# Reordering the opening loads of a four-layer kernel: fourth tile behind the seventh weight chunk

## Chip, cores, metric

One core of one Trainium2 chip. The metric is device time of one execution in microseconds (us), lower is better. The granted TensorE clock was 1.0, as a mean over the whole execution.

Engines: PE = TensorE matmul, DVE = VectorE, ACT = ScalarE, POOL = GpSimd, SP = SyncE, which issues all loads here (its queue shows as SPq).

## The reference, cut

Four layers over x of 2048 rows by 1024, bf16: linear attention, gated product, and both again. Each layer normalises its input first.

```python
x = x + _A_ref(_layernorm(x), A_wqkv, A_wo)          # phi(q), phi(k), kv = pk^T v, o = num / den, @ wo
x = x + _B_ref(_layernorm(x), w_gate, w_up, w_down)  # (x @ w_gate) * (x @ w_up) @ w_down
# ... and both once more
```

The change touches only the start of the first layer: loading x and the k weights, normalising the first four row tiles of 128 rows, and the first products.

## The kernel before

All loads go through one queue, in program order:

```python
load_x(0)
load_x(1)
for k in range(0, 3):
    load_k(k, k + 1)          # one 128x1024 chunk (256 KB) of the k weights
load_x(2)
load_k(3, 4)
load_x(3)
for k in range(4, 8):
    load_k(k, k + 1)
```

The first four tiles are only centred before their product; the reciprocal deviation is applied later, as a scale in the exponential on ACT. Tiles 0 and 1 are transposed on PE, 2 and 3 by DMA (`turn`). Two ways to a mean matter for tiles 2 and 3:

```python
def mean_by_halves(t, i):     # half on ACT, half on DVE
    nc.scalar.activation(out=junk[:, 0:NB], in_=X[:, t, 0:NB], func=ACT.Copy, scale=1.0 / D,
                         accum_out=part[:, i:i + 1])
    nc.vector.tensor_scalar(out=junk[:, NB:D], in0=X[:, t, NB:D], scalar1=1.0 / D, scalar2=0.0,
                            op0=ALU.mult, op1=ALU.add, accum_out=part[:, i + 1:i + 2])
# ... (cut)
mean_by_halves(2, 2)
centre_by_halves(2, 2)
turn(XN[:, 2, :], 0, 2)
ln_stats(3)                                  # the full statistics, on DVE
centre(3, stat[3][0][:, 0:1])
turn(XN[:, 3, :], 0, 3)
load_q()                                     # q weights, two loads of 1 MB
for t in range(4, NT):
    load_x(t)
for t in range(3):
    ln_stats(t)
for k in range(3, 6):
    for t in range(2):
        k_part(t, k, k + 1)                  # product of tile t with chunk k
for t in range(2):
    k_part(t, 6, 8)
k_part(2, 0, 8)
k_part(3, 0, 8)
# ... (cut) then q_unit(0): tile 0's q product, eight steps of two matmuls
```

## Time and profile before

| | us |
|---|---|
| median, first 3 runs | 1622.09 (1621.53 to 1622.28) |
| profiled span | 1620.1 |
| PE busy | 1607.5 (99%) |
| wait of PE at the fifth weight chunk | 0.38 in this trace |

The opening is the only part of this kernel where PE waits for a load at all; the lines that show it are in the prediction. How to read such a case: PE is the chain, so only PE's start-to-start gaps count, and a "true" wait below is a step less the 0.216 us that the prediction works out; the profile's own "idle before" is smaller by 0.16.

### The profile page before, as it was taken

The page shows a single profiled execution, that of the slowest core. Times are in us where ns is not written, and L with a number is a line of the kernel's source. Part 1 is how long each engine was busy: PE and PEld are TensorE (multiplying, and loading weights), DVE is VectorE, ACT ScalarE, POOL GpSimd, SP SyncE. Part 2 cuts the span into 40 slices and gives each one's busy share as a digit, 9 for nine tenths or more (in the row PEclk, how much of TensorE's full clock was granted, in tenths as well). Part 3 has the DMA queues.
Part 4 walks back from the last instruction along what each step waited for, and adds up shares of the span by engine and source line. Part 5 has one row for each costly group of instructions (what it writes and reads, how often), then busy time and mean ns, then how long its engine had stood idle before and what let it go on. Part 6 is the DMA issues. An engine that isn't in the chain of part 4 may idle for free.

```text
span 1620.1 us, 18047 instructions
## 1 busy us (share of the span) xinstructions
PE 1607.5 (99%) x7710; PEld 734.5 (45%) x7861; DVE 616.6 (38%) x946; ACT 284.0 (18%) x384; POOL 54.5 (3%) x135
## 2 busy tenths in 40 slices
PE   9999999999999999999999999999999999999999
PEld 4444444444444444444444444444444444444444
DVE  6899853202311321243255798432123113211111
ACT  5522201101110110011045231011011101101110
POOL 2100000000000000010000000000000000000000
DMA  8224856512650552142420257655236306521400
GB/s 247 53 72 93 246 162 176 162 52 60 171 159 0 147 162 81 52 156 66 92 52 1 78 114 219 181 157 165 69 102 175 127 20 173 165 66 65 156 1 26
DMA packets 236719, 183.10 MB, mean 113 GB/s; under 512 B 102368, under 2 KB 217312, under 8 KB 236640
## 3 DMA queue, kind: packets, MB, share of 16 engines
q1 hardware_dynamic: 236640, 181.95, 39.0%
q8 instruction: 61, 1.00, 0.3%
q14 instruction: 18, 0.15, 0.0%
HBM read 153.09 MB, written 4.19 MB: 97 GB/s over the span
## 4 chain that ended last, share of the span: by engine, by line
PE 99%; issue 1%; DMA 0%; SPq 0%; DVE 0%
PE ps L196 50%; PE ps L538 48%; PE ps L565 1%; DMA W<-in_A_wqkv_dram 0%; PE kv L306 0%; SPq L109 0%; PE pm L328 0%; PE ps L328 0%; DVE X L546 0%
## 5 line engine op out<-in xcount | busy, mean ns | idle before, releaser
L538 PE MATMUL ps<-xT,R 128*128 128x512 bf16 x2382 | 525.9, 379 | 2.6
L538 PEld LDWEIGHTS <-R 128*128 128x128 bf16 x2432 | 238.0, 98 | 286.9
L542 DVE TENSOR_TENSOR R<-gs,ps 128x512 bf16<-128x512 f32 x224 | 153.9, 687 | 533.5 <-ACT gs L541 533.5
L196 PEld LDWEIGHTS <-R 128*128 128x128 bf16 x2248 | 220.0, 98 | 265.2
L541 ACT COPY gs<-ps 128x512 f32<-128x512 f32 x224 | 131.3, 586 | 1040.2 <-PE ps L538 1011.5
L538 PE MATMUL ps<-xT,W 128*128 128x512 bf16 x1130 | 250.4, 379 | 1.2
L196 PEld LDWEIGHTS <-xT 128*128 128x128 bf16 x1536 | 149.5, 98 | 181.4 <-issue 1.9
L196 PE MATMUL ps<-W,xT 128*128 128x512 bf16 x997 | 222.8, 379 | 1.9 <-issue 0.3
L538 PEld LDWEIGHTS <-W 128*128 128x128 bf16 x1152 | 112.7, 98 | 135.9
L196 PE MATMUL ps<-W,R 128*128 128x512 bf16 x733 | 170.1, 379 | 0.8
L546 DVE TENSOR_TENSOR X<-X,ps 128x1024 bf16<-128x1024 bf16 (+3 forms) x34 | 39.4, 1158 | 335.8 <-PE ps L196 282.8
L196 PE MATMUL ps<-R,R 128*128 128x512 bf16 x506 | 111.8, 379 | 0.4
L196 PE MATMUL ps<-PQ,R 128*128 128x512 bf16 x488 | 111.4, 379 | 0.5
L196 PE MATMUL ps<-R,xT 128*128 128x512 bf16 x502 | 110.3, 379 | 0.5
L201 ACT ACTIVATE e<-ps 128x1024 bf16<-128x1024 f32 x56 | 57.3, 1024 | 141.2 <-PE ps L196 86.0
L175 DVE BATCH_NORM_STATS2 st<-X 128x6 f32<-128x512 bf16 x128 | 81.7, 680 | 0.1
L179 POOL TENSOR_SCALAR ve<-mv 128x1 f32<-128x1 f32 x64 | 16.2, 254 | 1325.8 <-DVE mv L177 1325.8
L196 PE MATMUL ps<-GL,R 128*128 128x512 bf16 x240 | 57.8, 379 | 0.3
L196 PE MATMUL ps<-xT,R 128*128 128x512 bf16 x240 | 57.5, 379 | 0.2
L378 DVE TENSOR_TENSOR X<-X,ps 128x1024 bf16<-128x1024 bf16 x32 | 38.7, 1209 | 17.0 <-PE ps L196 17.0
L186 DVE TENSOR_SCALAR R<-X,mv,rstd 128x1024 bf16<-128x1024 bf16 x64 | 33.7, 542 | 27.3 <-POOL rstd L181 24.0
L205 DVE TENSOR_SCALAR e<-e 128x1024 bf16<-128x1024 bf16 x64 | 26.9, 421 | 38.1 <-ACT e L201 38.1
(73 smaller groups left out, 456.6 us busy)
## 6 DMA issues: line engine op xcount, KB each, us to landing
R<-in_B_w_gate_dram SPq DMA_DIRECT2D x38, 1024.0 KB, 5.4
R<-in_B_w_up_dram SPq DMA_DIRECT2D x38, 1024.0 KB, 7.6
W<-in_B_w_gate_dram SPq DMA_DIRECT2D x18, 1024.0 KB, 5.4
W<-in_B_w_up_dram SPq DMA_DIRECT2D x18, 1024.0 KB, 7.6
W<-in_A_wqkv_dram SPq DMA_DIRECT2D x10, 1024.0 KB, 6.2
W<-in_B_w_down_dram SPq DMA_DIRECT2D x6, 1024.0 KB, 11.2
X<-in_A_x_dram SPq DMA_DIRECT2D x16, 256.0 KB, 6.7
PQ<-in_B_w_down_dram SPq DMA_DIRECT2D x4, 1024.0 KB, 8.4
```

The costliest lines, as they stand in the source:

```text
L175: nc.vector.bn_stats(out=st[:, c, :], in_=X[:, t, c * NB:(c + 1) * NB])
L179: nc.gpsimd.tensor_scalar(out=ve[:], in0=mv[:, 1:2], scalar1=1e-5, scalar2=None, op0=ALU.add)
L186: nc.vector.tensor_scalar(out=dst, in0=X[:, t, :], scalar1=mv[:, 0:1], scalar2=rstd[:], op0=ALU.subtract, op1=ALU.mult)
L196: nc.tensor.matmul(out=ps[:, n, :], lhsT=lhsT, rhs=rhs[:, n * NB:(n + 1) * NB], start=start, stop=stop)
L201: nc.scalar.activation(out=e[:], in_=flat(ps), func=ACT.Exp, **sc)
L205: nc.vector.tensor_scalar(out=e[:], in0=e[:], scalar1=1.0, scalar2=EPS, op0=ALU.min, op1=ALU.add)
L378: nc.vector.tensor_tensor(out=X[:, t, :], in0=X[:, t, :], in1=flat(ps), op=ALU.add)
L538: nc.tensor.matmul(out=ps[:, n, :], lhsT=w[:, k, j * P:(j + 1) * P], rhs=xT[g % 2][:, k, :], start=(k == 0), stop=(k == KD - 1))
L541: nc.scalar.copy(out=gs[:], in_=ps[:, 0, :])
L542: nc.vector.tensor_tensor(out=hT[:, f, :], in0=gs[:], in1=ps[:, 1, :], op=ALU.mult)
L546: nc.vector.tensor_tensor(out=X[:, t, a:b], in0=X[:, t, a:b], in1=ps, op=ALU.add)
L565: nc.tensor.matmul(out=ps[:, 0, 0:b - a], lhsT=hT[:, f, tl * P:(tl + 1) * P], rhs=wd[f][:, a:b], start=(f == 0), stop=(f == KF - 1))
```

## The change

Its intent: the wait at the fifth chunk comes from tile 3 standing ahead of it in the queue, so move tile 3 behind the seventh chunk; make up for its lateness with the quicker mean; use DVE's free time for tile 0's statistics; let the last steps of tiles 0 and 1 alternate, so that the eighth chunk is wanted later.

```diff
-    for k in range(0, 3):
+    for k in range(8):
         load_k(k, k + 1)
-    load_x(2)
-    load_k(3, 4)
-    load_x(3)
-    for k in range(4, 8):
-        load_k(k, k + 1)
+        if k in (2, 6):
+            load_x(2 if k == 2 else 3)
...
-            part = small.tile([P, 4], F32, tag="part", bufs=1, name="part")
+            part = small.tile([P, 6], F32, tag="part", bufs=1, name="part")
...
-            ln_stats(3)
-            centre(3, stat[3][0][:, 0:1])
+            ln_stats(0)
+            mean_by_halves(3, 4)
+            centre_by_halves(3, 4)
             turn(XN[:, 3, :], 0, 3)
...
-            for t in range(3):
+            for t in range(1, 4):
                 ln_stats(t)
-            for k in range(3, 6):
+            for k in range(3, 8):
                 for t in range(2):
                     k_part(t, k, k + 1)
-            for t in range(2):
-                k_part(t, 6, 8)
```

## The prediction

> **What bounds the kernel now.** I began with the page: is there anything but the matrix engine to win from?
>
> ```profile
> span 1620.1 us, 18047 instructions
> ...
> PE 1607.5 (99%) x7710; PEld 734.5 (45%) x7861; DVE 616.6 (38%) x946; ACT 284.0 (18%) x384; POOL 54.5 (3%) x135
> ...
> PE 99%; issue 1%; DMA 0%; SPq 0%; DVE 0%
> ```
>
> The first row gives the busy times, the last the chain that ended last. The chain is PE almost throughout, so a microsecond that PE loses or wins anywhere in the opening goes to the end undiminished, and nothing else counts. The diff touches the first 25 us only. So I next asked for the chain in the first 60 us (start, length, what):
>
> ```profile
> 4.48 5.72 DMA W<-in_A_wqkv_dram
> 10.20 0.04 issue
> 10.24 2.10 PE ps L196 x9
> 12.35 0.05 issue
> 12.40 10.74 PE ps L196 x49
> 23.14 0.05 issue
> 23.19 10.74 PE ps L196 x49
> ```
>
> Reader's points: a weight chunk issued at 4.48 lands at 10.20, PE starts on it at 10.24, and from there runs without a break. From 12.40 to 23.19 there are 49 records and one that is missing (each "issue 0.05" is such a hole), so one matmul takes 10.79 / 50 = 0.216 us. All waits of PE from 9 us to the end are these:
>
> ```profile
> PE ps L196 <- issue: 0.3, 2, 0.2
> PE ps L196 <- DMA W<-in_A_wqkv_dram: 0.2, 1, 0.2
> ```
>
> So one wait is left to remove, the one at 10.24. How long is it really? The timeline of PE before it:
>
> ```profile
> 7.92 2.10 PE L196 MATMUL ps<-W,xT 128*128 128x512 bf16 x9
> 10.24 0.38 PE L196 MATMUL ps<-W,xT 128*128 128x512 bf16 x1 [0.22 <-DMA W<-in_A_wqkv_dram]
> ```
>
> The profile counts 0.22 because it lets a matmul last 0.38, but the next could start 0.216 after the last. The ninth starts at 7.92 + 8 x 0.216 = 9.65, so the tenth could have started at 9.86: 0.38 us lost. That is the whole prize, 0.02% of the span.
>
> **What the skill says.** "TensorE: Matmul & The Clock Gate", Back-to-back issue gap, gives N/2.4 + 2.5 ns for a warm isolated gap, 215.8 ns at N = 512; the trace agrees (0.216). The lower sustained figure for N = 512 given there, about 131 ns, is not seen here. "DMA: Bandwidth & Descriptors", Queues, rings and completion order, says that each DMA engine consumes descriptors in ring order: with one issuing queue, to move a transfer in the queue is to exchange landing times. The trace agrees; the 256 KB transfers of the opening land one after another about 0.67 us apart. "Perfetto Trace Analysis", DMA Instruction — HWDGE, says that the recorded issue starts when its semaphores are satisfied and excludes the transfer: so I take landings, not the ends of issues.
>
> **The change part by part.**
>
> *Order of loads.* Issue times stay, since every one of the twelve transfers is 256 KB; contents change. Landings, as issue plus time to landing (queried issue by issue): slot 7 at 3.53 + 5.3 = 8.8, slot 8 at 4.01 + 5.5 = 9.5, slot 9 at 10.20, slot 10 at 4.96 + 5.9 = 10.9, slot 11 at 5.58 + 6.0, finer 11.53, slot 12 at 6.62 + 5.6 = 12.25. Before, tile 3 held slot 8 and the fifth to eighth chunks slots 9 to 12. After, the fifth chunk holds slot 8, the sixth 9, the seventh 10, tile 3 slot 11, and the eighth chunk keeps 12.
> PE wants the fifth at 9.86 (there at 9.5), the sixth four matmuls later at 10.72 (10.20), the seventh at 11.59 (10.9). With the k steps alternating, the eighth is wanted at 12.45 (12.25); by the old order, both last steps of tile 0 together, at 12.02, a wait of some 0.27. So alternation is needed, and adds no matmul. Gain: -0.38 us, with 0.2 us to spare at the tightest weight chunk.
>
> *Tile 2* is as before: its transpose is issued at 9.60 and lands 3.6 later at 13.2, wanted at 13.69 - 0.38 = 13.31. Just in time.
>
> *Tile 3's mean.* Tile 2 goes through the same code now, so its durations are known (DVE, then ACT):
>
> ```profile
> 8.21 0.69 DVE L415 TENSOR_SCALAR_CACHE_REDUCE junk<-X 128x512 bf16<-128x512 bf16 x1 [1.00 <-DMA X<-in_A_x_dram]
> 8.82 0.08 DVE L415 DVE_READ_ACCUMULATOR junk<-X 128x1 f32 x1
> 9.02 0.55 DVE L419 TENSOR_SCALAR R<-X,part 128x1024 bf16<-128x1024 bf16 x1
> 9.54 1.28 DVE L175 BATCH_NORM_STATS2 st<-X 128x6 f32<-128x512 bf16 x2
> 10.86 0.21 DVE L177 BATCH_NORM_AGGREGATE mv<-st 128x2 f32<-128x12 f32 x1
> 11.10 0.49 DVE L394 TENSOR_SCALAR R<-X,mv 128x1024 bf16<-128x1024 bf16 x1
> ```
>
> From the landing at 8.18 to the transpose at 9.60: 1.42 us. Tile 3 landed at 9.51 before, but its statistics and centring ran on DVE from 9.54 to 11.59. After, tile 0's statistics fill 9.54 to 11.07, tile 3 lands at 11.53, and its transpose is issued at 11.53 + 1.42 = 12.95 rather than 11.61: 1.34 later. It landed 3.1 after its issue; then 16.05, wanted at 17.15 - 0.38 = 16.77. In time, by 0.7.
>
> *Tile 0's statistics first* let ACT begin tile 0's exponential at about 13.1 instead of 14.02, where it waited for the reciprocal deviation. PE did not wait for that buffer before (nothing in its list), so this gives PE nothing; DVE ends its fourth statistics near 17.1 instead of 15.6, which PE does not see either.
>
> *What stands behind tile 3 in the queue.* The issuing queue takes its instructions in order:
>
> ```profile
> 9.60 3.25 SPq L190 DMA_TRANSPOSE xT<-R  x2
> 12.90 1.15 SPq L109 DMA_DIRECT2D W<-in_A_wqkv_dram  x2
> 14.09 1.26 SPq L109 DMA_DIRECT2D X<-in_A_x_dram  x2
> ```
>
> The two 1 MB halves of the q weights follow tile 3's transpose. The second is issued at 13.52, and the issue's own view has its landing:
>
> ```profile
> W<-in_A_wqkv_dram SPq DMA_DIRECT2D x1, 1024.0 KB, 7.7
> ```
>
> 13.52 + 7.7 = 21.2. The first lands at 12.90 + 5.6 = 18.5. Tile 0's q product wants the second for its fifth step. From 12.40: six matmuls to tile 2, 16 for tile 2, 16 for tile 3, 8 for q's first four steps: 12.40 + 46 x 0.216 = 22.33. Slack before: 1.1 us. After, both issues are 1.34 later, the halves land at 19.9 and 22.57, and PE, 0.38 earlier, wants them at 20.22 and 21.95. The first is in time; the second is late by 22.57 + 0.04 - 21.95 = 0.66 us.
>
> Sum: -0.38 + 0.66 = +0.28 us. I expect one wait to be exchanged for a longer one: 1622.09 + 0.28 = 1622.37, given as 1622.35.
>
> **The rivals.**
> 1. The q weights come in time and the whole 0.38 is kept: 1621.7. For it: the transposes of tiles 2 and 3 no longer overlap, so the engines may be quieter; in the 1 us windows from 14 to 16 us, traffic was only 100 and 266 GB/s, near 395 later, so something held the q weights back which the change may remove. Against: that weak stretch is just the end of tile 3's transpose (landing 14.76), which moves with it. Chance 1 in 4, partial recovery included.
> 2. Tile 3's transpose becomes the wait, if its landing takes over 3.8 us: +0.1 to +0.5 at tile 3, but this pushes PE towards the late q weights, and the two waits do not add: 1622.4 to 1622.6. Against: 3.1 in the profile here.
> 3. The eighth chunk or tile 2 slips by 0.1 to 0.2. Such a small wait also comes out of the later q wait, so the end is unchanged as long as the q wait stands: 1622.35 again.
> 4. The earlier exponential lets PE gain more. Against: no PE wait on ACT exists to remove.
>
> **Range and chances.** All branches lie within 1 us of the old time; the three runs of before spread over 0.75 us, more than the effect. So the range is 1621.6 to 1623.0, and a 2% move (32 us) would need something outside the opening, which the diff doesn't touch.
>
> **What would show it.** In the new profile: no wait at 10.24, PE dense from about 6.8 to 21.9; transposes issued near 9.60 and 12.95; the q loads issued near 14.24 and 14.86; then a PE wait on the wqkv load near 22, shown as about 0.5 (0.66 less the 0.16 that the modelled ends hide). Step 1 is wrong if a wait near 10 to 12 us remains; the last if PE runs through 22 us dense, and then the time should fall to about 1621.7.

## The result, and the profile after

| | median | runs |
|---|---|---|
| before, same rounds | 1621.95 | 6 (1621.53 to 1622.28) |
| after | 1622.35 | 6 (1621.78 to 1622.65) |

The ratio is 1.0002, 95% interval 0.9989 to 1.0015. Ratios are the mean time of one kernel's fast runs over that of the other's of the same rounds, so not quite the ratio of the medians. By the 2% measure nothing happened.

The queue of loads and transposes after (start, length, count), in answer to the one the prediction shows:

```profile
9.30 4.54 SPq L187 DMA_TRANSPOSE xT<-R  x2
13.89 1.15 SPq L109 DMA_DIRECT2D W<-in_A_wqkv_dram  x2
15.08 11.34 SPq L109 DMA_DIRECT2D X<-in_A_x_dram  x12
```

The q weights are issued at 13.89 in place of 12.90. This execution's opening loads ran about 0.3 us early (tile 2 landed at 7.88, before at 8.18), so relative to them the shift is the 1.3 us foretold. DVE, in answer to the lines of before:

```profile
9.19 1.28 DVE L172 BATCH_NORM_STATS2 st<-X 128x6 f32<-128x512 bf16 x2
11.22 0.69 DVE L412 TENSOR_SCALAR_CACHE_REDUCE junk<-X 128x512 bf16<-128x512 bf16 x1 [0.51 <-DMA X<-in_A_x_dram]
12.04 0.55 DVE L416 TENSOR_SCALAR R<-X,part 128x1024 bf16<-128x1024 bf16 x1
```

Tile 0's statistics come first, then DVE waits 0.51 us for tile 3, which lands at 11.19 and is centred for a transpose issued at 12.61: 1.42 us. And the waits of PE from 5 us to the end:

```profile
PE pt L400 <- DVE R L416: 0.5, 1, 0.5
PE ps L193 <- issue: 0.3, 2, 0.2
```

The wait at the fifth chunk is gone, as foretold, and the one for the q weights is not in the list either. The single matmul records show a step of 0.288 in place of 0.216 at the fifth q step, 22.11, just after the landing at 22.07: a wait of 0.07 us, too short for the list. Taken alone, this trace speaks for the prediction's first rival (q weights in time). But this profile is of the fastest of the six runs, 1621.78. A trace of a typical one was needed.

### The profile page after: what moved, and what is told of

Its sections match the earlier page's. It is cut to its first block, busy times and chain, and to the rows that moved or that the text cites. A ratio compares the mean times of both kernels' runs of the same rounds, so it can differ in the third digit from the quotient of the medians.

```text
span 1619.8 us, 18053 instructions
## 1 busy us (share of the span) xinstructions
PE 1607.8 (99%) x7710; PEld 734.8 (45%) x7861; DVE 616.9 (38%) x948; ACT 284.8 (18%) x386; POOL 54.1 (3%) x135
## 4 chain that ended last, share of the span: by engine, by line
PE 99%; issue 1%; DMA 0%; DVE 0%; DVEq 0%
PE ps L193 50%; PE ps L534 48%; PE ps L561 1%; PE kv L303 0%; DMA X<-in_A_x_dram 0%; PE pm L325 0%; PE pt L400 0%; PE ps L325 0%; DVE junk L412 0%; DVE R L416 0%; DVE X L542 0%; DVEq L416 0%
```

## The experiments

Theory (exchange): the wait for the fifth chunk was exchanged for one at the fifth step of tile 0's q product, whose weights stand in the queue behind tile 3's transpose. Rival: the two kernels are equal and 0.4 us is chance. Three calls, each on another chip and with its own runs of the kernel before (medians 1621.87 for e1 to e4, 1621.94 for e6 to e9, 1621.67 for e10 to e13, nine runs each). Every 95% interval of a ratio includes 1 (e8, a single run, has none); what is told apart here is told by medians and ranges within a call, and by the traces.

This table holds what all traces say (us from the span's start; a landing is that of a transfer, "q weights" the second half, or the third quarter where quartered; the wait is the start-to-start step less 0.216):

| kernel | first weight chunk | tile 3 | its transpose issued | q weights | fifth q step starts | wait there | span |
|---|---|---|---|---|---|---|---|
| before | 5.54 | 9.51 | 11.61 | 21.23 | 22.33 | 0 | 1620.1 |
| e8, before again | 6.40 | 9.79 | 11.89 | 21.49 | 22.59 | 0 | 1620.3 |
| after | 5.78 | 11.19 | 12.61 | 22.07 | 22.11 | 0.07 | 1619.8 |
| e1, after again | 5.68 | 11.89 | 13.30 | 22.66 | 22.70 | 0.50 | 1620.4 |
| e2, quarters | 5.35 | 11.65 | 13.06 | 21.13 | 21.99 | 0 | 1619.9 |
| e3, behind sixth | 5.08 | 10.28 | 11.70 | 21.24 | 21.85 | 0 | 1619.6 |
| e4, behind eighth | 6.19 | 12.48 | 13.90 | 23.33 | 23.37 | 0.89 | 1621.1 |
| e6, old mean | 5.84 | 12.04 | 14.14 | 23.62 | 23.66 | 0.89 | 1621.4 |
| e7, statistics late | 6.18 | 11.62 | 13.04 | 22.80 | 22.84 | 0.05 | 1620.6 |
| e9, sixth + quarters | 6.24 | 11.06 | 12.47 | 20.70 | 22.30 | 0 | 1620.2 |
| e10, sixth + pairs | 5.64 | 10.73 | 12.14 | 21.64 | 22.09 | 0 | 1619.8 |
| e11, sixth + late statistics | 5.78 | 11.25 | 12.67 | 22.39 | 22.43 | 0.02 | 1620.2 |
| e12, sixth again | 5.76 | 10.38 | 11.80 | 21.51 | 22.10 | 0 | 1619.8 |
| e13, old loads | 5.94 | 9.40 | 11.96 | 21.52 | 22.30 | 0 | 1620.0 |

Read it from the right: the span less the start of the fifth q step is 1597.7 to 1597.8 everywhere, but 1597.9 in the two with quarters. So that start is the time, and what sets it can be read off each trace.

**e1: the changed kernel again.** No edit.

> The changed kernel once more, for a second trace. Theory (exchange of waits): PE starts the fifth step of tile 0's q product 0.04 us after the second half of the q weights lands; the landing is tile 3's landing + 1.42 + 1.28 + 0.63 + 7.6 us. The first trace, of the fastest of six runs, shows a wait of only 0.07 us there because its opening loads ran 0.33 us early; another run should show 0.2 to 0.7 us. Time 0.2 to 0.5 us above the kernel before. Rival (the two kernels are equal, the 0.4 us between the medians is chance): a wait under 0.1 us again, and a time within 0.15 us of the kernel before.

Median 1622.45, 0.58 above the kernel before in the same rounds, a little over the 0.2 to 0.5 expected. The chain of this trace is the whole argument in one view:

```profile
5.70 6.19 DMA X<-in_A_x_dram
...
11.97 0.73 ACT junk L410 x2
12.70 0.03 issue
12.73 0.55 DVE R L416
13.27 1.21 DVE st L172 x2
14.48 0.05 SPq L187
14.53 0.05 issue
14.59 0.57 SPq L109
15.16 0.05 issue
15.21 7.45 DMA W<-in_A_wqkv_dram
22.66 0.04 issue
22.70 0.81 PE ps L193 x3
```

Tile 3's load, its half mean on ACT, its centring on DVE, the issue of its transpose, two issues of q weights, the transfer, and PE. The piece "DVE st" is put there by the inference from semaphores; the queue's own record has the transpose's issue in that stretch (13.30, 1.23 long, the least of any of the 94 such issues and nearly all of them that). PE's timeline has the wait:

```profile
22.70 0.59 PE L193 MATMUL ps<-W,xT 128*128 128x512 bf16 x2 [0.33 <-DMA W<-in_A_wqkv_dram]
```

The listed 0.33 is a true 0.50. Both things that the rival asked for failed: a wait under 0.1 and a time within 0.15. This opening also waited 0.46 us at the fourth chunk, which stands behind tile 2 in the queue, and tile 2 landed late (8.53): the opening differs from one execution to the next.

**e2: q weights in quarters.**

```diff
-            load_q()
+            for a in range(0, 8, 2):
+                load(wq[:, a:a + 2, :], wqkv_v[:, a:a + 2, 0:D])
```

> The q weights in four loads of 512 KB in place of two of 1 MB, so that the fifth step waits for the third quarter only. Theory: the third quarter lands about 0.7 to 1.3 us ahead of where the half landed, PE runs through the fifth step without a wait, the fourth quarter is in time for the seventh step (wanted 0.86 us later); time 0.2 to 0.5 us below the changed kernel in the same rounds, and at or below the kernel before. Rival (chance): no difference from the changed kernel beyond 0.15 us.

Median 1622.01: 0.44 below the changed kernel in the same rounds. PE's whole list from 12 us to the end has no wait for q:

```profile
PE ps L193 <- issue: 0.3, 2, 0.2
```

So the q weights do cost about what was said; this edit touches nothing that comes before them. It is not below the kernel before (1621.87). Its trace has 0.18 us more between the start of the last matmul and the end than the others (3.03 in place of 2.85), and e9, which has the quarters too, has the same. The single records put this after the last output has landed: 1.01 us from there to the end in place of 0.84, in which SyncE passes three closing semaphore waits, about 0.06 us each, where the kernel before and e12 have one. So it is no matter of moving data; why these waits come in another order, the record doesn't say.

**e3: tile 3 behind the sixth chunk.**

```diff
-        if k in (2, 6):
+        if k in (2, 5):
```

> Tile 3 behind the sixth weight chunk in place of the seventh. Theory: tile 3 lands 0.67 us earlier, so does its transpose's issue and the second half of the q weights: no wait at the fifth step. The seventh chunk lands 0.67 us later, at about 11.2 to 11.55, wanted at about 11.6: no wait or under 0.1 us. Time 0.2 to 0.5 us below the changed kernel. Rival (the weights' order is what costs): a wait at the seventh chunk of over 0.2 us and no gain.

Median 1621.77: 0.68 below the changed kernel, more than the 0.2 to 0.5 expected, and 0.10 below the kernel before. No wait over 0.03 us from 7 us on, neither at the seventh chunk nor at q. Its first chunk landed earliest of all, though, so it was repeated as e12.

**e4: tile 3 behind all chunks.**

```diff
-        if k in (2, 6):
+        if k in (2, 7):
```

> Tile 3 behind all weight chunks: the suspected cost doubled. Theory: transpose and q weights 0.67 us later than in the changed kernel, wait at the fifth step larger by 0.67 us, time 0.5 to 0.8 us above the changed kernel; tile 3's transpose lands at 16.4 to 16.8 against 16.8 wanted, so a small wait there may take a part of it, not added. Rival (the q weights are not what sets the time): within 0.2 us of the changed kernel.

Median 1622.98, 0.53 above the changed kernel, at the low end of what was expected. The chain has the same links as in e1, later:

```profile
7.15 5.33 DMA X<-in_A_x_dram
...
15.81 7.52 DMA W<-in_A_wqkv_dram
23.33 0.04 issue
23.37 0.81 PE ps L193 x3
```

The wait is 0.89 and PE also waits 0.21 at the first q step for the first half. The transpose landed at 17.00, wanted at 17.10: no wait there. Moving one 256 KB load by a slot moves the end: e3, e1 and e4 stand at 1621.77, 1622.45 and 1622.98 in the same rounds, and their ranges (1621.50 to 1622.06, 1622.13 to 1622.70, 1622.74 to 1623.24) do not overlap.

**e6: the old mean for tile 3.**

```diff
-            mean_by_halves(3, 4)
-            centre_by_halves(3, 4)
+            ln_stats(3)
+            centre(3, stat[3][0][:, 0:1])
...
-            for t in range(1, 4):
+            for t in range(1, 3):
```

> One part undone: tile 3's mean again from its full statistics on DVE, all else as in the changed kernel. Theory: from tile 3's landing to its transpose's issue 2.07 us (9.54 to 11.61 in the kernel before) in place of 1.42, so the q weights are 0.65 us later and PE's wait at the fifth q step is 0.65 us longer: time 0.5 to 0.8 us above the changed kernel (1622.42 in the last rounds), near 1623.0. Rival (the halves are of no use): within 0.2 us of the changed kernel.

Landing to transpose took 2.10 us in place of 1.41; median 1622.84. Against e1 that is 0.39 more, but of other rounds on another chip, where the kernel before stood 0.07 higher; the expectation of 0.5 to 0.8 was missed a little. Against e7 of the same rounds, which differs in the place of tile 0's statistics too, it is 0.60 more. The mechanism is in the trace: 0.89 at the fifth q step, 0.29 at the first, 0.12 at tile 3 (and 0.27 at the fourth chunk, before any of this). So the halves shorten the way from landing to transpose by what the trace of before says; the size in time rests on unlike comparisons.

**e7: tile 0's statistics not first.**

```diff
-            ln_stats(0)
             mean_by_halves(3, 4)
...
-            for t in range(1, 4):
+            for t in range(4):
                 ln_stats(t)
```

> One part undone: tile 0's statistics after tile 3's centring, all else as in the changed kernel. My prediction said that this part gives PE nothing. Theory now: it would have been wrong without it; tile 0's exponential then starts near 15.0 in place of 13.2, tile 0's PSUM buffer comes free near 17.2 to 17.6, tile 3's product is wanted at 16.9 to 17.0 and waits 0.2 to 0.6 us for ACT. The later wait for the q weights shrinks by as much, so the time stays within 0.15 us of the changed kernel. Rival (the prediction as written): no wait on ACT at tile 3's product.

```profile
17.61 0.59 PE L193 MATMUL ps<-W,xT 128*128 128x512 bf16 x2 [0.39 <-ACT R L199]
```

A wait of 0.55 us (0.39 in the list) on ACT, whose second pass over tile 0's PSUM buffer ended near 17.57:

```profile
16.46 1.11 ACT L199 ACTIVATE R<-ps,rstd 128x1024 bf16<-128x1024 f32 x1
```

The wait for q shrank to 0.05. Median 1622.24, against 1622.45 for the changed kernel: by the means (1622.29 and 1622.42) inside the 0.15, by the medians not, and not of the same rounds. In this trace the two waits in a row do not add: PE starts on the q weights 0.04 us after they land, as in e1. And my sentence that the statistics' order gives PE nothing was wrong for the trace: there was no such wait to remove, but the change would have made one. In time no gain from it is shown.

**e8: the kernel before again.** No edit, one run, state unknown.

> The kernel before once more, for a second trace of its opening. Theory: the wait at the fifth weight chunk is there again, between 0.1 and 0.6 us with the timing of the opening's loads, the second half of the q weights lands about 1 us before it is wanted, and the start of the fifth q step plus 1597.7 us is the span. Rival: no wait at the fifth chunk, it was chance.

1622.12. As expected, the wait at the fifth chunk (10.51) is there, 0.14 us only, too short for the list, and the q weights land 1.1 us before they are wanted. Here the first chunk landed at 6.40, in the other trace at 5.54; PE began its first weight matmul at 6.44 in place of 5.91 and had less to wait for later. So the 0.38 of the first trace is one value of something that varies.

**e9: both remedies.** The edits of e2 and e3 together.

> Tile 3 behind the sixth chunk and the q weights in quarters: the two remedies together. Theory: each alone removes the same wait, so together they give no more than the better one: within 0.15 us of tile 3 behind the sixth chunk (1621.77 in the last rounds), 0.5 to 0.7 below the changed kernel. Rival (in slower openings the halves still bind with tile 3 behind the sixth chunk): another 0.2 us or more.

Median 1622.16. No gain over e3 alone, but 0.39 above it in other rounds, where 0.15 was expected: missed, and so was "0.5 to 0.7 below the changed kernel" (0.29 below e1; 0.08 below e7 of the same rounds, which does wait). Part is the longer end (0.18). In the trace PE has no wait after 8 us; its opening started late (first chunk 6.24). That this is the rest for all five runs, one trace can't show.

**e12: tile 3 behind the sixth chunk again.** The edit of e3.

> Tile 3 behind the sixth chunk once more, as the base for the next two and for a second trace. The first trace had its first weight chunk at 5.08 us, early by 0.5 to 1.3 us against the other traces. Theory: PE has no wait from about 9 us on whatever the opening; with a first chunk near 6.2 PE starts its first weight matmul near 6.3 and the fifth q step at 22.1 to 22.3. Time 0 to 0.3 us below the kernel before, 0.4 to 0.7 below the changed kernel's 1622.42. Rival (the earlier gain was the luck of its opening): not below the kernel before, and a wait at the seventh chunk or at the q weights.

Median 1621.70, the kernel before 1621.67 in the same rounds: no gain on it, where 0 to 0.3 was expected. In the trace PE's whole list from 7 us to the end is

```profile
PE ps L193 <- issue: 0.3, 2, 0.2
```

(two gaps of 0.16 us, at 170.5 and 975.7 here, which ten of the fourteen traces have, the first of the kernel before too). Over both calls ten runs have mean 1621.75, the eighteen of before 1621.80. This version is better than the changed kernel, by 0.68 in the rounds they share (e3 and e1); against the kernel before it can't be told apart.

**e10: no alternation.** The edit of e3, and

```diff
-            for k in range(3, 8):
+            for k in range(3, 6):
                 for t in range(2):
                     k_part(t, k, k + 1)
+            for t in range(2):
+                k_part(t, 6, 8)
```

> The alternation undone (seventh and eighth steps of tile 0 together, then of tile 1), with tile 3 behind the sixth chunk so that no later wait can hide it. Theory: the eighth chunk is wanted 0.43 us earlier, at about 12.0 to 12.4, and lands at 11.7 to 12.5: a wait of 0 to 0.3 us with the opening's timing, and by as much slower than the base of the same rounds. Rival (the alternation is needed for more, or nothing): over 0.4 us, or a wait elsewhere.

Median 1621.74 against e12's 1621.70: not told apart. A wait at the eighth chunk is there, 0.50 us, more than the 0.3 that I allowed and than the 0.4 set for the rival:

```profile
PE ps L193 <- DMA W<-in_A_wqkv_dram: 0.3, 1, 0.3
```

Yet PE reached the fifth q step at 22.09, as in e12 (22.10): PE had come early to that chunk. What the alternation is worth stays open: the trace shows the wait, the medians (0.04 apart) no cost.

**e11: late statistics with tile 3 behind the sixth.** The edits of e3 and e7.

> Tile 0's statistics after tile 3's centring, with tile 3 behind the sixth chunk. With the late q weights the wait on ACT at tile 3's product (0.4 us) was absorbed. Theory: tile 3's centring ends 0.67 us earlier here, so the statistics do too: exponential from about 14.3, buffer free near 16.5, wanted near 16.7 to 16.9: no wait or under 0.1 us; time within 0.15 us of the base. Rival (statistics first matters by itself): a wait of 0.2 us or more at tile 3's product, and 0.2 us or more slower than the base.

Median 1621.84, 0.14 above e12: within what was expected, not resolved. The wait at tile 3's product was 0.12, a little more than 0.1. This trace also shows the price of the earlier slot: tile 3 landed late (11.25), the seventh chunk behind it at 11.90, and PE waited 0.26 us for that chunk, too short for the list (e10: 0.06). So with tile 3 behind the sixth chunk PE is not free of waits in every opening, as e12's expectation had it.

**e13: all but the order of loads.**

```diff
-        if k in (2, 6):
+        if k in (2, 3):
```

> All of the change but the order of the loads: tile 3 behind the fourth chunk as in the kernel before, its mean by halves, tile 0's statistics first, steps alternating. Theory: the wait at the fifth chunk is there again (0.1 to 0.4 us), the q weights come earlier than in the kernel before (about 0.6 us) but nobody waits for them: time within 0.15 us of the kernel before. Rival (the other parts are worth something alone, or cost something): more than 0.2 us off it.

Median 1622.04, the kernel before 1621.67: the expectation (within 0.15) was missed, and by the number its rival (over 0.2 off) holds. Two steps of the expectation failed in the trace. There was no wait at the fifth chunk: PE came to it at 10.22, after its landing at 10.06, because its first steps were slow:

```profile
5.98 0.89 PE L193 MATMUL ps<-W,xT 128*128 128x512 bf16 x2
6.71 0.61 PE L400 MATMUL pt<-ident,R 128*128 128x128 bf16 x8
```

In the trace of before these two rows start at 5.91 and 6.36: 0.45 apart in place of 0.73. In the single records PE's transposes start 0.106 us apart up to 5.5 here and 0.056 from 6.7 on, so PE works at about half rate at first. The full rate is there by 5.0 in e1 and by 5.4 in before, but here only after 6.4: besides the landings, a second thing that differs from one execution to the next.

And the q weights did not come earlier: tile 3 landed at 9.40, but its transpose was issued at 11.96, since tile 0's statistics now stood ahead of it on DVE. Neither explains 0.4 us. That the parts other than the order cost this much by themselves does not fit e12, which has them all and stands at 1621.70 in these rounds. The nine runs of before spread from 1621.20 to 1622.33, wider than in the others, so the difference may be chance. Open.

## Why the prediction was right

1622.35 was predicted and measured; that the two agree to the last digit is luck. The prediction added 0.28 to the 1622.09 of three runs; over six runs the kernel before has 1621.95, and the change added 0.40. The mechanism, one wait exchanged for a longer one further on, was right, as the traces and e2, e3 and e4 show. By its steps:

- *Wait at the fifth chunk removed*: shown in the trace after, where the four matmuls of each chunk follow without a gap. Its size, -0.38, is the term that was read off one trace. The second trace has 0.14, and with the q wait taken away (e3, e12) the kernel gains 0.05 us on the kernel before, not 0.38. PE started its first weight matmul between 5.5 and 6.4 us in these traces, and reached its full rate at different times (e13); a PE that is late anyway waits less at the fifth chunk, so removing that wait gains less.
- *Tile 3's transpose 1.42 us after its landing*: 1.42 and 1.41. In time for its product: landed at 15.70 and 16.40, wanted at 16.86 and 17.03.
- *q weights shifted with it and late by 0.66*: shown, by the chain in e1 and by e2, e3 and e4, which move the landing and with it the time. The waits traced are smaller, 0.07 and 0.50: the transfer took 7.55 and 7.45 from issue to landing in place of 7.7, and in e1 PE had already lost 0.46 at the fourth chunk. In time, taking the lateness away gave 0.44 (e2) and 0.68 (e3) in the rounds shared with e1; the term is about right.
- *Sum +0.28*: +0.40 and +0.58 between the medians. With the terms as the runs have them, a cost of 0.44 to 0.68 less a gain of 0.05 gives 0.39 to 0.63: the net was predicted low because the gain was taken too large.
- *Tile 0's statistics give PE nothing*: wrong in the mechanism, as e7's trace showed; without this part PE would have waited 0.55 us for ACT. Since that wait came out of the later one, the sum did not suffer.
- *Small waits ahead of a later fixed one do not add* (rival 3): e7's trace shows it, and e1's, with its 0.46 at the fourth chunk.
- Rival 1 (q weights in time) is in one trace all but true (0.07), which is why a profile of the fastest run would have misled; e1, e2 and e4 settled it. What it guessed of the transfer is partly so: 7.45 to 7.55 in place of 7.7. Rival 2 did not occur.
- The view of tile 2's mean in the prediction is headed "DVE, then ACT" but shows DVE alone; its sum of 1.42 does not need the rest.

## What to carry to other kernels

When a load is moved back in a single queue, follow what its consumer issues on that same queue: here a 256 KB tile delayed its transpose, and the transpose delayed 2 MB of weights needed 10 us later. Read the size of an opening wait from more than one trace, since the first loads land at different times in each execution. A slot earlier is not free either: it delays the chunk that gives way (e11). And profile a typical run before explaining a difference: the one at hand may be the fastest.

## What the Trainium skill lacked or had wrong

- "TensorE: Matmul & The Clock Gate", Back-to-back issue gap: the sustained spacing of about 131 ns for N = 512 with alternating weight loads is not reached here; PE, dense for tens of microseconds with a weight load about as often as a matmul (7861 and 7710), keeps 216 ns, its isolated figure.
- "DMA: Bandwidth & Descriptors", DMA Transpose (X-bar): it gives no issue time for a trn2 transpose of this shape. Here it holds the queue 1.23 us (128x1024 bf16) against 0.43 us for a 256 KB load, and that delay falls on everything behind it.
- "DMA: Bandwidth & Descriptors", Latency and other measured facts: nothing on how much the first transfers of a program vary. The first weight chunk, always issued at about 1.65, landed between 5.08 and 6.40 us.
